# Normalising the query feature map ahead of the numerator matmul, on one core: half the columns there, a new round trip, and a hand-placed order

## The chip, the cores and the metric

One core of one Trainium2 chip. The metric is the device time of one execution in microseconds; lower is better. Most executions of one kernel agree within about 0.3%. The program uses one core only. "Span" is the time from the first to the last recorded instruction; the device time is about 2 us longer.

Engines are named as in the profile: PE is TensorE (matmul), PEld its weight loads, DVE is VectorE, ACT ScalarE, POOL GpSimd, SP the engine that issues most DMAs.

## The reference, cut to what matters

```python
xn = layernorm(x)                                  # x: 2048 tokens x 512
# A: linear attention with 32 heads of 16 ("hedgehog")
q, k, v = split(xn @ wqkv)
pq, pk  = q @ w_phi, k @ w_phi                     # per head, 16 x 16
phi_q   = concat(softmax(pq), softmax(-pq))        # 32 features per head
phi_k   = concat(softmax(pk), softmax(-pk))
kv, z   = phi_k^T @ v, sum over tokens of phi_k
o       = (phi_q @ kv) / (phi_q @ z + 1e-6)
A       = o @ wo
# B: gated unit without an activation
B       = ((xn @ w_gate) * (xn @ w_up)) @ w_down   # F = 1792
out     = x + A + B
```

## The kernel before

All work is in bf16 with f32 accumulation. There are 16 token tiles of 128 (index n) in four groups of 4 (index T). The parts that the change and the argument touch (names are the kernel's own):

```python
# G: one of 56 blocks of the gated unit; ps_gu is a pool of three banks of PSUM, the memory that the matmuls write
gps = ps_gu.tile([P, TT], F32, name="gu")
... 4 matmuls of 512 columns ...
nc.scalar.copy(out=g_sb[:], in_=gps[:])                       # ACT frees the gate's bank
ups = ps_gu.tile([P, TT], F32, name="gu")
... 4 matmuls of 512 columns ...
nc.vector.tensor_tensor(out=hT[T][:, f, :], in0=ups[:], in1=g_sb[:], op=ALU.mult)   # DVE frees it

# Pq: query features of a whole group, features on partitions; NOT normalised
... 4 matmuls: lhsT=W1q, rhs=xnT (512 tokens) ...
nc.scalar.activation(out=Es[T][:, 0, cq, :], in_=pq[:], func=AF.Exp, scale=1.0)
nc.scalar.activation(out=Es[T][:, 1, cq, :], in_=pq[:], func=AF.Exp, scale=-1.0)

# ND: numerator and denominator of one token tile. J = DH + 2 = 18 columns per head:
# 16 of kv, one of z, and one of ones that yields the softmax sum
for cq in range(CQ):
    for s in (1, 0):                                           # exp(-p) and exp(p) apart
        nc.tensor.matmul(nd[...], lhsT=Es[T][:, s, cq, ...], rhs=KVZ[:, s, cq], ...)  # 8 heads x 18 = 144 columns
... DVE: reciprocal (rsm), ratio (rho), multiply (tmp), add (sm), reciprocal (rden) ...
nc.gpsimd.tensor_tensor(out=o_tok, in0=sm, in1=rden, op=ALU.mult)
... o_tok is stored to DRAM (od) and loaded back transposed into oT ...

# KVZ is cleared and its ones are set in the head, on POOL
nc.gpsimd.memset(KVZ[:], 0.0)
... 8 small copies ...
```

The other blocks: LNs, LNr, LNx are the layer norm of a tile (statistics on DVE, rstd on ACT, the scaling on DVE); PK, EX (exps), RED, RCP, PHI (DVE sums, reciprocal, normalising multiply) and VV and KV make kv and z; Fin is the last projection of a tile. In a loop over the key tiles these blocks are mixed with G; then a second loop does ND, the next group's Pq, and G or Fin. Instructions run on each engine in the order in which the program places them.

The softmax here doesn't subtract the row's maximum and nothing guards it: scores larger than these inputs give would overflow.

Of the kernel before, what the change touches and what calls it, by code (L numbers as in the profile page):

```python
# [8 lines left out]
BF16 = mybir.dt.bfloat16  # L9
F32 = mybir.dt.float32  # L10
AF = mybir.ActivationFunctionType
# [10 lines left out]
def kernel(  # L22
# [12 lines left out]
    nc = tc.nc  # L35
# [10 lines left out]
    J = DH + 2  # L46
# [11 lines left out]
    wT_pool = ctx.enter_context(tc.tile_pool(name="wT", bufs=1))  # L58
# [17 lines left out]
    KVZ = wpool.tile([P, 2, CQ, HC, J], BF16, name="KVZ")  # L76
# [8 lines left out]
    wkT = wT_pool.tile([P, DC, D], BF16, name="wT")  # L85
# [7 lines left out]
    nc.sync.dma_start_transpose(out=wkT[:], in_=A_wqkv[:, D:2 * D])  # L93
# [28 lines left out]
    BD = wT_pool.tile([P, DC, HC, DH], BF16, name="BD")  # L122
# [3 lines left out]
    nc.gpsimd.memset(KVZ[:], 0.0)  # L126
    for s in range(2):
        for cq in range(CQ):
            nc.gpsimd.tensor_copy(out=KVZ[:, s, cq, :, DH + 1:DH + 2], in_=BO16[:, :, 0:1])

# [46 lines left out]
    a2e = ctx.enter_context(tc.tile_pool(name="a2e", bufs=2))  # L177
    Es = {}

    def Pq(T, cq, pool, tag):  # L180
        if cq == 0:
            Es[T] = a2e.tile([P, 2, CQ, TT], BF16, name="E")
        pq = pool.tile([P, TT], F32, name=tag, **({"bufs": 2} if tag == "pk" else {}))
        for j in range(DC):
            nc.tensor.matmul(pq[:], lhsT=W1q[:, j, cq * P:(cq + 1) * P], rhs=xnT[:, j, T * TT:(T + 1) * TT],  # L185
                             start=(j == 0), stop=(j == DC - 1))
        nc.scalar.activation(out=Es[T][:, 0, cq, :], in_=pq[:], func=AF.Exp, scale=1.0)  # L187
        nc.scalar.activation(out=Es[T][:, 1, cq, :], in_=pq[:], func=AF.Exp, scale=-1.0)

    with tc.tile_pool(name="ln", bufs=4) as lnpool, \  # L190
# [10 lines left out]
        def LNs(n):  # L201
            ng, ni = divmod(n, GT)
            if ni == 0:
                xns[ng] = xnpool.tile([P, GT, D], BF16, name="xn")
            stats = lnpool.tile([P, nc.vector.BN_STATS_DIM], F32, name="stats")
            nc.vector.bn_stats(out=stats[:], in_=xall[:, n, :])  # L206
            mv = mvs[n] = lnpool.tile([P, nc.vector.BN_AGGR_DIM], F32, name="mv")
            nc.vector.bn_aggr(out=mv[:], in_=stats[:])
# [91 lines left out]

        LNs(0)
# [29 lines left out]
        wqT = wT_pool.tile([P, DC, D], BF16, name="wT")  # L331
        ln_s = [(4, 5), (6, 7)] + [(m,) for m in range(8, 16)] + [(), ()]
        for n in range(NT):
            st = ln_s[min(n + 1, 11)]
            xm = ln_s[min(n, 11)]
            RED(n)
            G()
            if n >= GT:
                VV(n)
            if 12 <= n:  # L340
                foldj(wqT, W1q, n - 12, ps_a1.tile([P, D], F32, name="pk", bufs=2)[:])
            if n > 0:
                KV(n - 1)
            for m in xm:
                LNr(m)
            for m in xm:
                LNx(m)
                if m % 2 == 1:
                    TRst(m)
            if n == 8:  # L350
                nc.sync.dma_start_transpose(out=wqT[:], in_=A_wqkv[:, 0:D])
                nc.sync.dma_start(out=wd[:], in_=B_w_down.rearrange("(c p) d -> p c d", p=P))
                nc.sync.dma_start(out=wo[:], in_=A_wo.rearrange("(c p) n -> p c n", p=P))
            RCP(n)
            PHI(n)
            G()
            for m in st:
                LNs(m)
            if n == GT - 1:
                G()  # L360
            if n + 1 < NT:
                PK(n + 1)
                EX(n + 1)
            if n != GT - 1:
                G(2 if n == 2 else 1 if n < NT - 3 else 0)
        Pq(0, 0, ps_a1, "pk")
        G()
        KV(NT - 1)
        H4 = HC // 2
        kvr = kvt[:].rearrange("p (c r) w -> p c r w", r=2)  # L370
        for s in range(2):
            for r in range(2):
                src, dst = slice(s * HW, (s + 1) * HW), slice(r * HW, (r + 1) * HW)
                mk = BO16[src, s * H4:(s + 1) * H4, :]
                m16 = _bcast_ap(mk, [mk.ap[0], [0, CQ], [DH, H4], [1, DH]])
                m8 = _bcast_ap(mk, [mk.ap[0], [0, CQ], [DH, H4]])
                nc.vector.tensor_tensor(out=KVZ[dst, s, :, r * H4:(r + 1) * H4, 0:DH],
                                        in0=kvr[src, :, r, 0:HW].rearrange("p c (h d) -> p c h d", d=DH),
                                        in1=m16, op=ALU.mult)
                nc.vector.scalar_tensor_tensor(out=KVZ[dst, s, :, r * H4:(r + 1) * H4, DH],  # L380
                                               in0=kvr[src, :, r, HW:HW + 1].to_broadcast((HW, CQ, H4)),
                                               scalar=0.5e-6, in1=m8, op0=ALU.add, op1=ALU.mult)
        Pq(0, 1, ps_a1, "vp")
        Pq(0, 2, ps_a1, "pk")
        Pq(0, 3, ps_gu, "gu")
        G()

    with tc.tile_pool(name="a2s", bufs=2) as a2s, \
            tc.tile_pool(name="a2o", bufs=3) as a2o, \
            tc.tile_pool(name="ps_pq", bufs=1, space=PSUM) as ps_pq, \  # L390
            tc.tile_pool(name="ps_nd", bufs=1, space=PSUM) as ps_nd:
        ods = {}

        def ND(n):
            T, t4 = divmod(n, GT)
            nd = ps_nd.tile([P, 2, 2, 512], F32, name="nd")
            for cq in range(CQ):
                hf, cl = divmod(cq, 2)
                for s in (1, 0):
                    nc.tensor.matmul(nd[:, s, hf, cl * HC * J:(cl + 1) * HC * J],  # L400
                                     lhsT=Es[T][:, s, cq, t4 * P:(t4 + 1) * P],
                                     rhs=KVZ[:, s, cq].rearrange("p h j -> p (h j)"),
                                     start=True, stop=True)
            ndv = [nd[:, s, :, 0:2 * HC * J].rearrange("p a (h j) -> p a h j", j=J) for s in range(2)]
            rsm = a2s.tile([P, 2, 2 * HC, 1], F32, name="rsm")
            nc.vector.reciprocal(out=rsm[:], in_=ndv[1][:, :, :, DH + 1:DH + 2])
            rho = a2s.tile([P, 2, 2 * HC, 1], F32, name="rho")
            nc.vector.tensor_tensor(out=rho[:], in0=ndv[0][:, :, :, DH + 1:DH + 2], in1=rsm[:], op=ALU.mult)
            tmp = a2s.tile([P, 2, 2 * HC, DH + 1], F32, name="tmp")
            nc.vector.tensor_tensor(out=tmp[:], in0=ndv[1][:, :, :, 0:DH + 1],  # L410
                                    in1=rho[:].to_broadcast((P, 2, 2 * HC, DH + 1)), op=ALU.mult)
            sm = a2s.tile([P, 2, 2 * HC, DH + 1], F32, name="sm")
            nc.vector.tensor_tensor(out=sm[:], in0=ndv[0][:, :, :, 0:DH + 1], in1=tmp[:], op=ALU.add)  # L413
            rden = a2s.tile([P, 2, 2 * HC, 1], F32, name="rden")
            nc.vector.reciprocal(out=rden[:], in_=sm[:, :, :, DH:DH + 1])  # L415
            o_tok = a2o.tile([P, D], BF16, name="o_tok")
            nc.gpsimd.tensor_tensor(out=o_tok[:].rearrange("p (a h d) -> p a h d", a=2, d=DH),  # L417
                                    in0=sm[:, :, :, 0:DH],
                                    in1=rden[:].to_broadcast((P, 2, 2 * HC, DH)), op=ALU.mult)
            if t4 == 0:  # L420
                ods[T] = dpool.tile([TT, D], BF16, name=f"od{T}")
            nc.sync.dma_start(out=ods[T][t4 * P:(t4 + 1) * P, :], in_=o_tok[:])
            if t4 == GT - 1:
                nc.sync.dma_start_transpose(out=oT[:, :, T * TT:(T + 1) * TT], in_=ods[T][:])

        fin_next = 0
        for n in range(NT):
            T, t4 = divmod(n, GT)
            ND(n)
            pq = (lambda: Pq(T + 1, t4, ps_pq, "pq")) if T + 1 < NT // GT else None  # L430
            if pq is not None:
                pq()
            if n == GT + 1:
                G()
            if n > GT:
                Fin(fin_next)
                fin_next += 1
            else:
                G(2 if n == 0 else 1)
        while fin_next < NT:  # L440
            Fin(fin_next, 2 if fin_next == NT - 1 else 1)
            fin_next += 1
# [28 lines left out]
```

## Time and profile before

| | before |
|---|---|
| device time, median (lowest to highest, 5 runs) | 227.84 us (227.75 to 228.79) |
| span of the profiled run | 226.1 us |
| PE busy, DVE busy, ACT busy | 97%, 67%, 38% |

From the page of the kernel before: busy time of each engine with its share of the span; then for 40 equal slices of the span the busy tenths of DVE (9 is 90% or more); then the chain of work that ended last, by engine.

```profile
PE 219.5 (97%) x1238; PEld 108.2 (48%) x1261; DVE 152.0 (67%) x263; ACT 86.0 (38%) x177; POOL 22.5 (10%) x42
...
DVE  4769998887779777655877569975555557752121
...
PE 86%; DVE 8%; issue 3%; DMA 1%; ACT 1%; DVEq 0%
```

PE is busy 97% of the span. DVE is full only in six of the slices, three of them early (4 to 6). The chain says what binds: 86% of the span is PE work, and most of the rest is in the head.

A busy PE need not run at its peak, because matmuls are pipelined, so I read PE from start to start in its timeline. Its columns are: start, duration from the first start to the last end, engine, source line, operation, output<-inputs, shape, count. First an ND block and the Pq block after it, then a KV block and the G block after it (kernel before):

```profile
141.36 0.67 PE L400 MATMUL nd<-KVZ,E 128*128 128x144 bf16 x8
141.87 0.81 PE L185 MATMUL pq<-xnT,W1q 128*128 128x512 bf16 x3
```

```profile
95.11 0.42 PE L298 MATMUL kv<-vt,phik 128*128 128x65 bf16 x8
95.37 0.81 PE L151 MATMUL gu<-xnT,wg 128*128 128x512 bf16 x2
```

Four matmuls of 512 columns start every 0.863 us (216 ns each). ND holds PE from 141.36 to 141.87 us, thus 0.50 us for eight matmuls of 144 columns, 62.5 ns each. KV holds it from 95.11 to 95.37, thus 0.26 us for eight of 65 columns.

From the groups of instructions by line and shape (source line, engine, operation, out<-in, shapes, count | busy us, mean ns | idle before, releaser):

```profile
L400 PE MATMUL nd<-KVZ,E 128*128 128x144 bf16 x128 | 10.6, 226 | 0.1
...
L282 DVE TENSOR_REDUCE sums<-e 128x64 f32<-128x1024 f32 x16 | 19.3, 1209 | 3.3 <-ACT e L268 3.3
```

L400 is ND; L282 is RED, which reduces 1024 elements in 1.21 us.

### The profile page before, as it was taken

To read this page: it belongs to the slowest core of one execution; us is meant where nothing else is said; L and a number is where in the kernel's file an instruction comes from. 1 tells how busy PE (TensorE), PEld (TensorE's weight loads), DVE (VectorE), ACT (ScalarE), POOL (GpSimd) and SP (SyncE) were. 2 spreads that over 40 slices of the span, in tenths; PEclk is the share of its full clock that TensorE was granted. 3 is DMA by queue.
4 is the path that set the end of the run, shared out by engine and by line. 5 is a ranking of instruction groups with operands and counts; after the bars stand their busy time and mean duration, and the time that the engine had idled before them with its cause. 6 is when DMAs were issued, how large, how long until landed. Compare 5 with 4: busy or idle time off the path is not lost.

```text
span 226.1 us, 3293 instructions
## 1 busy us (share of the span) xinstructions
PE 219.5 (97%) x1238; PEld 108.2 (48%) x1261; DVE 152.0 (67%) x263; ACT 86.0 (38%) x177; POOL 22.5 (10%) x42
## 2 busy tenths in 40 slices
PE   7899999999999999999999999999999999999994
PEld 2354444444444444445444454544555455554453
DVE  4769998887779777655877569975555557752121
ACT  4575553455454554445455745431111110000000
POOL 6200000000000000000000011330221111130000
PEclk9999999999999999999999999999999999999999
DMA  5999440101407924000000001073142115215201
GB/s 152 268 374 372 138 94 0 51 0 46 93 3 181 339 82 96 0 0 0 4 0 0 0 4 46 31 88 93 46 108 80 46 66 145 74 46 118 69 26 46
DMA packets 33825, 19.38 MB, mean 86 GB/s; under 512 B 20112, under 2 KB 32784, under 8 KB 33808
## 3 DMA queue, kind: packets, MB, share of 16 engines
q1 hardware_dynamic: 33280, 19.14, 30.6%
q8 instruction: 10, 0.16, 0.3%
q10 hardware_dynamic: 528, 0.02, 0.1%
q14 instruction: 7, 0.06, 0.1%
HBM read 8.67 MB, written 5.77 MB: 64 GB/s over the span
## 4 chain that ended last, share of the span: by engine, by line
PE 86%; DVE 8%; issue 3%; DMA 1%; ACT 1%; DVEq 0%
PE gu L169 21%; PE gu L151 18%; PE gu L157 18%; PE gu L172 6%; PE vp L273 5%; PE pk L259 5%; PE pq L185 4%; PE nd L400 4%; DVE hT L159 2%; DVE stats L206 2%; PE kv L298 2%; DVE xn L217 1%; DVE sums L282 1%; DMA xall<-in_A_x_dram 1%; PE pk L185 1%
## 5 line engine op out<-in xcount | busy, mean ns | idle before, releaser
L157 PE MATMUL gu<-xnT,wu 128*128 128x512 bf16 x223 | 57.3, 379 | 0.1
L151 PE MATMUL gu<-xnT,wg 128*128 128x512 bf16 x215 | 56.6, 379 | 0.6
L169 PE MATMUL gu<-wd,hT 128*128 128x512 bf16 (+1 forms) x235 | 50.8, 366 | 0.2
L159 DVE TENSOR_TENSOR hT<-gu,g_sb 128x512 bf16<-128x512 f32 x56 | 38.4, 686 | 15.9 <-PE gu L157 13.3
L154 ACT CAST g_sb<-gu 128x512 bf16<-128x512 f32 x56 | 33.0, 590 | 21.6 <-PE gu L151 21.0
L174 DVE TENSOR_TENSOR o_sb<-gu,xall 128x512 bf16<-128x512 f32 (+1 forms) x17 | 11.2, 660 | 36.2 <-PE gu L172 34.1
L169 PEld LDWEIGHTS <-hT 128*128 128x128 bf16 x238 | 23.1, 98 | 24.4
L417 POOL TENSOR_TENSOR o_tok<-sm,rden 128x512 bf16<-128x512 f32 x16 | 16.9, 1058 | 179.4 <-DVE rden L415 176.1
L157 PEld LDWEIGHTS <-wu 128*128 128x128 bf16 x224 | 21.9, 98 | 26.4
L151 PEld LDWEIGHTS <-wg 128*128 128x128 bf16 x224 | 20.8, 98 | 23.1 <-issue 0.8
L282 DVE TENSOR_REDUCE sums<-e 128x64 f32<-128x1024 f32 x16 | 19.3, 1209 | 3.3 <-ACT e L268 3.3
L187 ACT ACTIVATE E<-pq 128x512 bf16<-128x512 f32 x12 | 7.2, 597 | 35.4 <-PE pq L185 31.2
L293 DVE TENSOR_TENSOR phik<-e,rs 128x1024 bf16<-128x1024 f32 x16 | 19.6, 1225 | 0.5
L267 ACT ACTIVATE e<-pk 128x512 f32<-128x512 f32 x16 | 9.6, 597 | 18.3 <-PE pk L259 17.1
L172 PE MATMUL gu<-wo,xnT 128*128 128x512 bf16 (+1 forms) x66 | 16.3, 366 | 0.1
L259 PE MATMUL pk<-W1k,xnT 128*128 128x512 bf16 x63 | 16.2, 379 | 0.1
L273 PE MATMUL vp<-wv,xnT 128*128 128x512 bf16 x54 | 13.9, 379 | 0.1
L275 ACT CAST vt<-vp 128x512 bf16<-128x512 f32 x14 | 8.2, 587 | 13.8 <-PE vp L273 11.6
L413 DVE TENSOR_TENSOR sm<-nd,tmp 128x544 f32<-128x544 f32 x16 | 11.6, 725 | 1.5
L206 DVE BATCH_NORM_STATS2 stats<-xall 128x6 f32<-128x512 bf16 x16 | 10.8, 678 | 2.2 <-DMA xall<-in_A_x_dram 2.2
L410 DVE TENSOR_TENSOR tmp<-nd,rho 128x544 f32<-128x544 f32 x16 | 11.6, 724 | 0.5
L185 PE MATMUL pq<-xnT,W1q 128*128 128x512 bf16 x43 | 11.7, 379 | 0.2
(63 smaller groups left out, 157.7 us busy)
## 6 DMA issues: line engine op xcount, KB each, us to landing
od<-o_tok SPq DMA_DIRECT2D x16, 128.0 KB, 1.7
out_dram<-o_sb SPq DMA_DIRECT2D x15, 128.0 KB, 1.7
wd<-in_B_w_down_dram SPq DMA_DIRECT2D x1, 1792.0 KB, 10.3
xall<-in_A_x_dram SPq DMA_DIRECT2D x3, 512.0 KB, 12.0
xd<-xn SPq DMA_DIRECT2D x6, 256.0 KB, 2.4
wg<-in_B_w_gate_dram SPq DMA_DIRECT2D x1, 1024.0 KB, 8.3
wu<-in_B_w_up_dram SPq DMA_DIRECT2D x1, 1024.0 KB, 10.5
wv<-in_A_wqkv_dram SPq DMA_DIRECT2D x1, 512.0 KB, 4.8
```

The source lines that it names most:

```text
L151: nc.tensor.matmul(gps[:], lhsT=wg[:, c, f * P:(f + 1) * P], rhs=xnT[:, c, T * TT:(T + 1) * TT], start=(c == 0), stop=(c == DC - 1))
L154: nc.scalar.copy(out=g_sb[:], in_=gps[:])
L157: nc.tensor.matmul(ups[:], lhsT=wu[:, c, f * P:(f + 1) * P], rhs=xnT[:, c, T * TT:(T + 1) * TT], start=(c == 0), stop=(c == DC - 1))
L159: nc.vector.tensor_tensor(out=hT[T][:, f, :], in0=ups[:], in1=g_sb[:], op=ALU.mult)
L169: nc.tensor.matmul(fin[:], lhsT=hT[T][:, f, t4 * P:(t4 + 1) * P], rhs=wd[:, f, sl], start=(f == 0), stop=False)
L172: nc.tensor.matmul(fin[:], lhsT=oT[:, c, n * P:(n + 1) * P], rhs=wo[:, c, sl], start=False, stop=(c == DC - 1))
L185: nc.tensor.matmul(pq[:], lhsT=W1q[:, j, cq * P:(cq + 1) * P], rhs=xnT[:, j, T * TT:(T + 1) * TT], start=(j == 0), stop=(j == DC - 1))
L259: nc.tensor.matmul(pk[:], lhsT=xnT[:, j, n * P:(n + 1) * P], rhs=W1k[:, j, :], start=(j == 0), stop=(j == DC - 1))
L273: nc.tensor.matmul(vp[:], lhsT=xnT[:, j, n * P:(n + 1) * P], rhs=wv[:, j, :], start=(j == 0), stop=(j == DC - 1))
L282: nc.vector.tensor_reduce(out=sums[:], in_=ev, axis=AX.X, op=ALU.add)
L293: nc.vector.tensor_tensor(out=phik[:].rearrange("p k (h f) -> p (k h) f", f=DH), in0=ev, in1=rss[n][:].to_broadcast((P, 2 * H, DH)), op=AL ...
L417: nc.gpsimd.tensor_tensor(out=o_tok[:].rearrange("p (a h d) -> p a h d", a=2, d=DH), in0=sm[:, :, :, 0:DH], in1=rden[:].to_broadcast((P, 2 ...
```

## The change: its intent, and the diff

The intent is to make ND cheaper for PE. Queries are treated as keys already were: tokens on partitions, and normalised before the product. Then exp(p) and the scaled exp(-p) of four heads fill the 128 rows of one weight load, the two halves add up inside the matmul, and the column of ones is not needed: 4 heads x 17 = 68 columns instead of 144. In exchange the features must be transposed, by a store to DRAM and a transposing load (`qd`, `qT`), as o_tok's are. To hide that round trip, and to place the new DVE work, the loops are replaced by one hand-written list of block names. Cut to the core:

```diff
-    J = DH + 2
+    J = DH + 1
-    KVZ = wpool.tile([P, 2, CQ, HC, J], BF16, name="KVZ")
+    KVZ = wpool.tile([P, 2 * CQ, H4, J], BF16, name="KVZ")
-    nc.gpsimd.memset(KVZ[:], 0.0)
-    for s in range(2):
-        for cq in range(CQ):
-            nc.gpsimd.tensor_copy(out=KVZ[:, s, cq, :, DH + 1:DH + 2], in_=BO16[:, :, 0:1])
+    MK = consts.tile([P, H4], BF16, name="MK")          # a mask, used once when KVZ is written
+        def PQ(n):   # 4 matmuls: lhsT=xnT tile, rhs=W1q; then
+            nc.scalar.activation(out=phiq[:, :, 0, :], in_=pqv, func=AF.Exp, scale=1.0)
+            nc.scalar.activation(out=eq[:], in_=pqv, func=AF.Exp, scale=-1.0)
+        def QR(n):
+            nc.vector.tensor_reduce(out=sq[:, 0, :]..., in_=phiqs[n][:, :, 0, :]..., op=ALU.add)
+            nc.vector.tensor_reduce(out=sq[:, 1, :], in_=eqs[n][:]..., op=ALU.add)
+            nc.vector.reciprocal(out=rq[:], in_=sq[:, 1, :])
+            nc.vector.tensor_tensor(out=rho[:]..., in0=sq[:, 0, :], in1=rq[:], op=ALU.mult)
+            nc.gpsimd.tensor_tensor(out=phiqs[n][:, :, 1, :]..., in0=eqs[n][:]..., in1=rho[:]..., op=ALU.mult)
+            nc.sync.dma_start(out=qds[T][...], in_=phiqs[n][:]...)
+            if t4 == GT - 1:                            # two transposing loads per group of four tiles
+                for u in range(2):
+                    nc.sync.dma_start_transpose(out=qTs[T][...], in_=qds[T][...])
+        def ND(n):
+            for i in range(KB):
+                nc.tensor.matmul(nd[:, i, 0:H4 * J], lhsT=qTs[T][:, i, ...], rhs=KVZ[:, i]..., ...)  # 68 columns
+            nc.vector.reciprocal(out=rden[:], in_=ndv[:, :, :, DH:DH + 1])
+            nc.vector.tensor_tensor(out=o_tok[:]..., in0=ndv[:, :, :, 0:DH], in1=rden[:]..., op=ALU.mult)
 ... (the same store and transposing load of o_tok) ...
-        for n in range(NT):  ... the two loops, Pq, the old ND ...
+        for t in (
+            "S6 A1 E0 G W S7 L4 G L5 L6 L7 G C0 G E1 G A2 S8 C1 E2 G K0 G A3 D1 K1 C2 G E3 G L8 "
+ ... (list cut) ...
+            "R7 K13 E15 C15 K14 G G P8 P9 K15 B G N0 G R8 G N1 G G N2 R9 G G N3 G P10 G P11 R10 N4 "
+ ... (list cut) ...
+            "F F F N12 G G N13 G N14 F N15 F F F F F F F ").split():
```

In the list S is LNs, L is LNr and LNx, A is PK and EX, E is RED, C is RCP and PHI, K is KV, V is VV, D a fold of W1q, P is PQ, R is QR, N is ND, F is Fin, B the writing of KVZ, W and X late weight loads.

## The prediction

> **What bounds it now.** TensorE's stream. On the page PE is 97% busy and the chain of waits is 86% PE, at full granted clock. In the timeline of PE, matmuls with 512 columns start 216 ns apart (four take 0.863 us) almost without a break: first G blocks to the last Fin, added up at these intervals, give 207.4 us, and the trace has about 207.8 us. Only some 0.4 us is stall. DVE is busy 67%, ACT 38%, POOL 10%.
>
> **What changes, from TensorE's side.** GLU, Fin, PK, VV, KV, PQ and the folds keep their count and columns. Only ND changes: eight matmuls of 144 columns (0.50 us from first start to the next block's start in the timeline, 62.5 ns each) become eight of 68. KV already runs eight of 65 columns in 0.26 us, so I estimate 0.27 us. Saving: 16 x 0.23 = 3.7 us. The Trainium skill, "TensorE: Matmul & The Clock Gate", section "Back-to-back issue gap", gives N/2.4 + 2.5 ns: 62.5 ns for 144 (the trace agrees) and about 31 ns for 68 (the trace's 32.5 ns for 65 is slightly above). That saving is all on the critical path.
>
> **DVE.** Removed per token tile: two reciprocals, rho, tmp, sm (353+347+191+724+725 ns). Added: two 512-element sums, reciprocal, product (about 1.86 us of DVE time), and in ND a reciprocal and the o_tok multiply (0.98 us). The sums are estimated from the existing 1024-element sum (1209 ns); the skill's "VectorE: DVE Perf Modes", tier table, keeps reductions at 1x whatever the type, so bf16 input doesn't help. DVE busy rises from 152 to about 159 us. POOL keeps a 1.06 us multiply per tile. DMA gains 16 stores and 8 transposes; transposes land in 4 to 6 us now and the list leaves them more.
>
> **Where it could be given back.** The new hand-placed order pulls Q work into the first half. Running sums along the list: DVE work and PE work stay within about 3 us of each other from 15 to 105 us (DVE almost full). At each block that needs a DVE result (PSUM buffers of G, KV after PHI), the largest shortfall is 0.6 us. That assumes DVE never waits; its waits for ACT (rstd up to 1.15 us each before) have no room now, so I add about 1 us. After 110 us DVE has ample room.
>
> **Prediction.** 227.84 - 3.7 + about 1.1 = 225.2 us, range 223.9 to 227.2. Faster by over 2% needs under 223.3 us, more than the whole ND saving, hence 0.07; within 2% 0.90; slower by over 2% 0.03.
>
> **What would show it.** Right: ND's eight matmuls take about 0.27 us; PE's busy time falls by about 4 us in total and every other PE group keeps its mean; the timeline shows a few PE gaps, below 2 us in sum, all between 20 and 105 us, released by DVE (hT) or by ACT behind DVE; DVE over 90% busy there; tail unchanged. Wrong: ND intervals well above 35 ns; PE gaps over 3 us; PE waiting for qT or oT transposes, or for wqT at the first fold; reductions or POOL's multiply clearly slower.
>
> **What would make it wrong.** The queue on SP blocking (phiq stores wait on POOL, transposes on stores) so that late loads reach TensorE late; contention between POOL's strided multiply and DVE; several DVE waits in the full stretch adding up to 3 us or more, leaving no gain.

## The result, and the profile after

| | before | after |
|---|---|---|
| device time, median | 227.84 us (15 runs) | 223.37 us (8 runs, 223.2 to 223.93) |
| ratio, 95% interval | | 0.9794 (0.9778 to 0.981) |
| span of the profiled run | 226.1 us | 221.9 us |
| first G block to the start of the last matmul group | 209.98 us | 205.96 us |

Ratios here are the mean time of one kernel's runs over that of the other's of the same rounds, so not quite the ratio of the medians quoted. Executions over 1.5% slower than the fastest of the same kernel are left out of the means. The gain is 2%, on the edge of what the verdict calls faster (its word here is "unclear" between faster and the same); 223.37 us lies below the predicted range.

The last row of the table is used throughout. I call it the stretch: the time in the PE timeline from the first G matmul to the start of the last group of Fin matmuls. (In every profile the first G group shows three of its four matmuls, as records can be missing, so I put its start one interval, 0.216 us, before the first recorded one.) The stretch leaves out the head, which varies by about a microsecond from run to run, and it repeats well: 205.96 us in three profiles of the changed stream. The two ends, in the kernel before and in the changed kernel (222.64 - 12.88 + 0.216 = 209.98 us; 218.44 - 12.70 + 0.216 = 205.96 us):

```profile
12.88 0.81 PE L151 MATMUL gu<-xnT,wg 128*128 128x512 bf16 x3
...
222.64 0.60 PE L172 MATMUL gu<-wo,xnT 128*128 128x256 bf16 x4
```

```profile
12.70 0.81 PE L151 MATMUL gu<-xnT,wg 128*128 128x512 bf16 x3
...
218.44 0.60 PE L172 MATMUL gu<-wo,xnT 128*128 128x256 bf16 x4
```

The changed kernel's page, the same lines as before:

```profile
PE 215.1 (97%) x1238; PEld 104.6 (47%) x1261; DVE 156.0 (70%) x273; ACT 85.8 (39%) x177; POOL 20.5 (9%) x34
...
DVE  4669999999999999999988696546556136312121
...
PE 95%; DMA 2%; issue 1%; SPq 1%; DVE 0%; ACT 0%; ACTq 0%
```

DVE is now at 9 tenths from slice 4 to slice 20, and PE is as full as before. The chain is 95% PE.

An ND block of the changed kernel in the timeline of PE:

```profile
114.83 0.42 PE L331 MATMUL kv<-KVZ,qT 128*128 128x68 bf16 x8
115.08 1.02 PE L151 MATMUL gu<-xnT,wg 128*128 128x512 bf16 x4
```

ND holds PE for 0.25 to 0.26 us (114.83 to 115.08) instead of 0.50, as estimated from KV. Sixteen times 0.245 us are 3.9 us.

Groups of the changed kernel by line and shape:

```profile
L331 PE MATMUL kv<-KVZ,qT 128*128 128x68 bf16 x128 | 6.7, 194 | 0.0
...
L282 DVE TENSOR_TENSOR phik<-e,rs 128x1024 bf16<-128x1024 f32 x16 | 20.7, 1294 | 0.6
...
L306 DVE TENSOR_REDUCE sq<-phiq 128x32 f32<-128x512 bf16 x16 | 10.8, 675 | 0.0
L309 DVE TENSOR_REDUCE sq<-eq 128x32 f32<-128x512 f32 x16 | 10.8, 675 | 0.0
```

L331 is ND. L306 and L309 are the two new sums; the bf16 one takes 675 ns like the f32 one. The Trainium skill, "VectorE: DVE Perf Modes", section "The perf-mode tier table", lists tensor_reduce at 1x for every type, and the trace agrees. L282 is PHI, 1225 ns on average before and 1294 now (see the end).

Now the full stretch of DVE, by windows (columns: window, its length, then busy us and count of PE, PEld, DVE, ACT, POOL; granted clock; DMA share; GB/s). First the kernel before, then the changed kernel:

```profile
34.00:60.00 26.00, 25.73 (x146) 12.19 (x147) 21.68 (x34) 12.36 (x28) 0.00 (x0) 1.00 0.16 41
60.00:90.00 30.00, 29.84 (x164) 14.20 (x167) 24.50 (x36) 15.54 (x34) 0.00 (x0) 1.00 0.48 132
90.00:105.00 15.00, 14.89 (x86) 7.21 (x87) 9.84 (x13) 7.13 (x13) 0.00 (x0) 1.00 0.00 0
```

```profile
34.00:60.00 26.00, 25.84 (x155) 12.71 (x157) 25.57 (x43) 16.82 (x39) 0.00 (x0) 1.00 0.41 118
60.00:90.00 30.00, 29.84 (x178) 14.41 (x180) 29.28 (x48) 18.42 (x39) 4.24 (x4) 1.00 0.43 105
90.00:105.00 15.00, 14.71 (x88) 7.04 (x88) 14.62 (x22) 8.79 (x17) 2.92 (x3) 1.00 0.10 37
```

From 34 to 105 us DVE is busy 69.5 of 71 us (98%) against 56.0 before. PE's busy time there is the same within 0.1 us. So DVE has filled up and PE has lost nothing.

Was DVE held up by ACT, as I had feared? From the view of who waited for whom (us in total, times, longest), the kernel before and the changed kernel:

```profile
DVE xn L217 <- ACT rstd L213: 6.5, 6, 1.2
```

```profile
DVE xn L206 <- ACT rstd L202: 0.6, 2, 0.3
```

The waits of LNx for rstd did not hurt: they shrank from 6.5 to 0.6 us.

In total: the stretch is 4.02 us shorter. Of that 3.9 us is ND, and the rest, 0.1 us, is all the change that stalls of PE made. An estimate says the same: the matmuls of the built programs in the stretch are 894 of 512 columns, 32 of 256, 16 of 128, 128 of KV and 128 of ND; at the intervals read in the traces (0.863 us for four of 512; 0.109, 0.055 and 0.0325 us for one of the next three; for one of ND 0.0625 before against 0.032 after) they add up to about 209.4 and 205.5 us, so that only some 0.5 us of the stretch is stall, before and after. The median span over all runs of the first batch below is 226.2 us before and 221.4 after, so 4.8 us shorter; 4.0 of them are the stretch and about 0.8 the head. The time outside the span is about 0.2 us longer (223.50 - 221.4 = 2.1 us, against 228.06 - 226.2 = 1.9).

### The profile page after: what moved, and what is told of

It reads as the page before. It is cut to its first block, busy times and chain, and to the rows that moved or that the text cites. A ratio compares the mean times of both kernels' runs of the same rounds, so it can differ in the third digit from the quotient of the medians.

```text
span 221.9 us, 3359 instructions
## 1 busy us (share of the span) xinstructions
PE 215.1 (97%) x1238; PEld 104.6 (47%) x1261; DVE 156.0 (70%) x273; ACT 85.8 (39%) x177; POOL 20.5 (9%) x34
## 4 chain that ended last, share of the span: by engine, by line
PE 95%; DMA 2%; issue 1%; SPq 1%; DVE 0%; ACT 0%; ACTq 0%
PE gu L157 22%; PE gu L169 22%; PE gu L151 21%; PE gu L172 6%; PE pk L295 6%; PE pk L248 6%; PE vp L262 6%; DMA wv<-in_A_wqkv_dram 2%; PE kv L331 2%; PE kv L287 2%; PE pk L262 1%; SPq L81 1%; PE pk L235 1%; PE gu L213 0%; DVE o_sb L174 0%
## 5 line engine op out<-in xcount | busy, mean ns | idle before, releaser
L151 PE MATMUL gu<-xnT,wg 128*128 128x512 bf16 x213 | 55.9, 379 | 0.5
L159 DVE TENSOR_TENSOR hT<-gu,g_sb 128x512 bf16<-128x512 f32 x56 | 37.7, 684 | 9.6 <-PE gu L157 9.5
L316 POOL TENSOR_TENSOR phiq<-eq,rho 128x512 bf16<-128x512 f32 x16 | 17.0, 1060 | 140.9 <-DVE rho L314 69.5
L282 DVE TENSOR_TENSOR phik<-e,rs 128x1024 bf16<-128x1024 f32 x16 | 20.7, 1294 | 0.6
L300 ACT ACTIVATE phiq<-pk 128x512 bf16<-128x512 f32 x16 | 9.6, 598 | 21.5 <-PE pk L295 14.6
L295 PE MATMUL pk<-W1q,xnT 128*128 128x512 bf16 x62 | 16.0, 379 | 0.1
L262 PE MATMUL vp<-wv,xnT 128*128 128x512 bf16 x56 | 14.4, 379 | 1.5 <-DMA wv<-in_A_wqkv_dram 1.2
L337 DVE TENSOR_TENSOR o_tok<-kv,rden 128x512 bf16<-128x512 f32 x16 | 11.1, 691 | 0.6
L306 DVE TENSOR_REDUCE sq<-phiq 128x32 f32<-128x512 bf16 x16 | 10.8, 675 | 0.0
L309 DVE TENSOR_REDUCE sq<-eq 128x32 f32<-128x512 f32 x16 | 10.8, 675 | 0.0
```

The costliest lines, as they stand in the source:

```text
L151: nc.tensor.matmul(gps[:], lhsT=wg[:, c, f * P:(f + 1) * P], rhs=xnT[:, c, T * TT:(T + 1) * TT], start=(c == 0), stop=(c == DC - 1))
L262: nc.tensor.matmul(vp[:], lhsT=xnT[:, j, n * P:(n + 1) * P], rhs=wv[:, j, :], start=(j == 0), stop=(j == DC - 1))
L282: nc.vector.tensor_tensor(out=phik[:].rearrange("p k (h f) -> p (k h) f", f=DH), in0=ev, in1=rss[n][:].to_broadcast((P, 2 * H, DH)), op=AL ...
L295: nc.tensor.matmul(pq[:], lhsT=xnT[:, j, n * P:(n + 1) * P], rhs=W1q[:, j, :], start=(j == 0), stop=(j == DC - 1))
L316: nc.gpsimd.tensor_tensor(out=phiqs[n][:, :, 1, :].rearrange("p k (h f) -> p k h f", f=DH), in0=eqs[n][:].rearrange("p k (h f) -> p k h f" ...
```

## The experiments

Theories. A: PE's stream is the only bound; the gain is ND's columns plus a shorter head, and the full DVE costs nothing because of *when* PE needs its results and which PSUM buffer each G block gets. B, the prediction's: the full DVE stretch costs about 1 us, hidden by something else. Twelve runs. They ran in three batches on three chips, each beside runs of the kernel before: after_again, fixed_rot, dve_less and wv_early; nd128, dve_more, old_order and before_kvz; the other four.

### after_again: the changed kernel once more

No edit.

> The changed kernel once more, as the yardstick for the runs beside it. Every theory: 223.2 to 223.9 us, ratio to the kernel before 0.978 to 0.982. In the profile: first G block at about 12.5 us and the eight ND matmuls about 0.26 us, as in its first profile.

Measured: 223.5 us (223.36 to 224.45), ratio 0.9808 (0.9785 to 0.9831); stretch 205.96 us again. The first G is at 13.0 us instead of 12.5 in the profiled run, because wv landed 0.5 us later. So the head varies and the stretch doesn't: differences of a few tenths are read from the stretch below.

### nd128: is the gain the columns?

```diff
-  nc.tensor.matmul(nd[:, i, 0:H4 * J], ..., rhs=KVZ[:, i]..., ...)           # 68 columns
+  nc.tensor.matmul(nd_flat[i*128 - pad : (i+1)*128 - pad], ..., rhs=KVZ_flat[i*68 - pad : i*68 - pad + 128], ...)
+  # pad is 60 for the last i, else 0; the other 60 columns are never read
```

> The changed kernel with every ND matmul widened from 68 to 128 columns; the additional columns are never read, the result stays right. Theory A (the gain is the columns that TensorE streams in ND): 128 matmuls x 60 columns / 2.4 = 3.2 us more, so about 226.5 us, and ND's eight start within 0.45 us instead of 0.26. Theory B (the gain came from the new order or the head, and short matmuls are bound by something else than columns): under 1 us more.

Measured: 226.48 us (226.36 to 226.57), ratio 0.9918; stretch 209.09 us, 3.13 us more. Result right. An ND block and what follows, in its timeline of PE:

```profile
114.47 0.61 PE L332 MATMUL kv<-KVZ,qT 128*128 128x128 bf16 x8
114.91 1.03 PE L151 MATMUL gu<-xnT,wg 128*128 128x512 bf16 x4
```

Eight matmuls of 128 columns hold PE 0.44 us, 55 ns each. The Trainium skill, "TensorE: Matmul & The Clock Gate", section "Back-to-back issue gap", gives N/2.4 + 2.5 ns as the gap of an isolated matmul, 55.8 ns for 128 columns; the trace agrees with it even in this stream (the page has more for streams, see the end). Columns in ND cost PE their full length, one for one, in the time. Theory A holds for this part.

### dve_less: what does the full DVE cost?

```diff
-  nc.vector.tensor_reduce(out=sq[:, 0, :]..., in_=phiqs[n][:, :, 0, :]..., ...)
-  nc.vector.tensor_tensor(out=rho, in0=sq[:, 0, :], in1=rq[:], op=ALU.mult)
+  nc.vector.tensor_tensor(out=rho, in0=sq[:, 1, :], in1=rq[:], op=ALU.mult)   # wrong result on purpose
```

> Result wrong on purpose: the first of the two sums of each Q tile is left out, 16 x 0.6 us less VectorE work, 11 of it before 111 us. Theory A (TensorE's stream bounds everything, the full VectorE costs next to nothing): VectorE busy falls from 156 to about 145 us and the time falls by at most 0.3 us. Theory B (as predicted: the full VectorE stretch costs about 1 us): the time falls by 0.7 to 1.2 us.

Measured: 223.07 us (223.01 to 223.57), 0.43 us less than after_again, ratio 0.9785. The profiled run's first G was 1.25 us earlier than after_again's (wv had landed earlier), so the time alone can't tell; the stretch is 205.78 us, 0.18 us less. DVE busy fell from 156.0 to 147.6 us. So taking 8.4 us of work from DVE gains the changed kernel about 0.2 us. All stalls of PE in the stretch are some 0.5 us by the estimate above, in both kernels; the prediction had charged 1.1 us more for DVE.

### dve_more: then is DVE far ahead?

```diff
   nc.vector.reciprocal(out=rs[:]..., in_=sums[:])
+  if n in range(4, 14):
+      nc.vector.reciprocal(out=rs[:, 0:H]..., in_=sums[:, 0:H])     # the same values again
```

> The changed kernel with one more 32-element reciprocal on VectorE (0.35 us) after each of ten reciprocals of K tiles 4 to 13, inside the stretch where VectorE is full: 3.5 us more VectorE work. Result right. Theory A (no stall was seen because the list has filled VectorE exactly to what TensorE leaves it, with about 0.5 us to spare): 1.5 to 3.3 us longer, gaps of TensorE at KV and at gates between 60 and 105 us. Theory B (VectorE runs far enough ahead of what TensorE needs from it that its being 98% busy means nothing): at most 0.5 us longer.

Measured: 226.46 us (226.4 to 226.51), ratio 0.9917; stretch 209.08 us, 3.12 us more for about 3.5 us of DVE work. Result right. PE's timeline near the first stalls:

```profile
62.05 1.03 PE L157 MATMUL gu<-xnT,wu 128*128 128x512 bf16 x4
63.66 0.43 PE L289 MATMUL kv<-vt,phik 128*128 128x65 bf16 x8 [0.58 <-DVE phik L284]
```

The KV block should start at 62.91 us, four intervals after 62.05; it starts at 63.66, and the profile names PHI (DVE phik) as what it waited for. In all, the view of waits counts 1.4 us for KV behind PHI in two waits, and 0.2 us for an up group behind an hT. Another 0.9 us, at 103.6 and 105.0 us, are two waits of PE for banks that ACT frees; the first of the exps there had itself waited 2.1 us for PHI. So both statements are true: DVE's load is nearly free as it stands, and there is almost nothing to spare. Ten times 0.35 us came back as 3.1 us. Theory B is wrong about the cost and right about the edge.

### fixed_rot, before_fixed, fixed_less: who frees the PSUM bank

My running sum had found a shortfall of 0.6 us: a gate (the first four matmuls of a G block) needed a bank that DVE had not yet freed. It assumed that the three banks go round in strict turn; then every gate gets the bank of the up matmuls two G blocks earlier, which DVE's hT frees. The trace of the changed kernel contradicts that. PE, then DVE:

```profile
59.82 1.03 PE L151 MATMUL gu<-xnT,wg 128*128 128x512 bf16 x4
...
61.81 1.02 PE L151 MATMUL gu<-xnT,wg 128*128 128x512 bf16 x4
...
64.66 1.03 PE L151 MATMUL gu<-xnT,wg 128*128 128x512 bf16 x3
```

```profile
64.79 1.28 DVE L159 TENSOR_TENSOR hT<-gu,g_sb 128x512 bf16<-128x512 f32 x2
```

The G blocks start at 59.82, 61.81 and 64.66 us. The two hT in the second fence are those of the first two blocks. The earlier one ends at about 65.4 us, but the third block's gate starts at 64.66: it isn't in that bank. The built program says the same; these are rows of its PE order at that block, with the engine that each matmul waits for:

```
584 L151 Matmult gu<-xnT,wg 128x512 [waits Activation_49]
...
592 L157 Matmult gu<-xnT,wu 128x512 [waits DVE_49]
```

The pool handed out a bank that ACT had freed (from the previous gate), and the DVE-freed one went to the up matmuls 0.86 us later. Ten of the 56 gates are served so in the changed kernel, six in the kernel before. The test is to force strict turns, in the changed kernel (fixed_rot), in the kernel before (before_fixed), and together with the lighter DVE (fixed_less):

```diff
-  ps_gu = ctx.enter_context(tc.tile_pool(name="ps_gu", bufs=3, space=PSUM))
+  # three pools' worth of one buffer each, taken in turn by a small wrapper:
+  return ps_gu0.tile(shape, dt, name=f"gu{'abc'[i]}")     # i = 0, 1, 2, 0, ...
```

> The changed kernel with the three PSUM buffers of the G blocks handed out in strict rotation, as my running sum had assumed; in the build as it stands five late gates get a buffer that ScalarE frees instead of one that VectorE frees. Theory A (the hand-out is why the 0.6 us shortfall of the prediction never came): the gate at 30.5 us must now wait for an hT multiply that ended at 30.85 us, the one at 64.66 us for one that ended at 65.40 us, so TensorE stalls by about 0.4 us and 0.8 us in all, and the time is 0.5 to 1.0 us longer than the changed kernel's. Theory B (my VectorE durations were too long and VectorE was simply ahead): no gap, within 0.15 us.

> Control for the strict rotation: the kernel before with its three G buffers handed out in strict rotation. There 6 of 56 gates take a buffer freed by ScalarE, 5 of them in the first 30 us. Theory A (rotation costs only where VectorE is behind, and in the kernel before it is behind for the first 35 us alone): the stretch from first G to last Fin grows from 210.0 us by 0.2 to 1.2 us, less than half of the 2.7 us that rotation cost the changed kernel. Theory B (rotation as such costs, whatever the order): it grows by 2 to 3.5 us.

> Strict rotation and the left-out sum together (result wrong on purpose). Theory A (rotation costs because VectorE is behind when its buffer is due): with 0.6 us less VectorE work per Q tile the cost of rotation shrinks; the stretch from first G to last Fin is 206.2 to 207.7 us, against 208.7 with rotation alone and 205.8 with the lighter VectorE alone. Theory B (rotation costs for another reason): 208.3 us or more.

Measured:

| stretch, us | banks as the build hands them out | strict turns | difference |
|---|---|---|---|
| kernel before | 209.98 | 210.47 (before_fixed) | 0.49 |
| changed kernel | 205.96 | 208.70 (fixed_rot) | 2.74 |
| changed kernel, lighter DVE | 205.78 (dve_less) | 206.20 (fixed_less) | 0.42 |

Times: fixed_rot 226.53 us (226.06 to 227.09), ratio 0.993, 3.0 us over after_again; fixed_less 223.66 us, ratio 0.9834; before_fixed 228.91 us against 227.81 of the kernel before on the same chip, ratio 1.0043 (1.0019 to 1.0067), of which 0.5 us is the stretch; the rest is in the head, whose first G is 0.86 us later in that profile than in the kernel before's. One of fixed_less's six runs took 226.56 us and the others 223.5 to 224.1; the stretch is from one of the others. The same place in fixed_rot, all engines:

```profile
64.57 1.02 PE L257 MATMUL pk<-W1k,xnT 128*128 128x512 bf16 x4
...
65.58 0.68 DVE L168 TENSOR_TENSOR hT<-gub,g_sb 128x512 bf16<-128x512 f32 x1
...
66.31 1.02 PE L160 MATMUL gub<-xnT,wg 128*128 128x512 bf16 x3 [0.71 <-DVE hT L168]
```

PK runs until 65.43 us, and the gate follows only at 66.31, named as waiting 0.71 us for hT, which ran from 65.58 in the bank `gub`. This is exactly the wait that the prediction had foreseen, and more of them came later (at 124, 135 and 165 us): 2.7 us in all, not the 0.5 to 1.0 that I expected. It needs both: strict turns and a DVE that is behind. With 0.6 us less DVE work per query tile it shrinks to 0.4 us, and in the kernel before, whose DVE has room after 35 us, it is 0.5 us.

### old_order: what the list is for

The blocks of the changed kernel, in the order of the kernel before (all key tiles first, then each query tile one group ahead of its ND):

```diff
-  "... L12 K5 P0 S14 S15 G R0 P1 C7 ... B G N0 G R8 G N1 G G N2 ..."
+  "... P0 G K15 B R0 P1 R1 P2 R2 P3 R3 G N0 P4 R4 G G N1 P5 R5 G N2 P6 R6 G N3 P7 R7 G N4 ..."
```

> The arithmetic of the changed kernel, in the order of the kernel before: all K tiles first, then Q tiles one group ahead of their ND. Theory A (the order's part is to hide the new round trip of phi_q: exp, sums, multiply on GpSimd, store, transposing load, some 11 us from the last PQ of a group to its first ND): TensorE waits 5 to 9 us at the ND that opens each of the four groups, and the time is 15 to 35 us longer than the changed kernel's, slower than the kernel before. Theory B (the order matters little, fewer ND columns are the whole change): within 2 us of 223.4 us.

Measured: 283.26 us (283.17 to 284.69), ratio 1.2425. From the view of who waited for whom:

```profile
PE kv L331 <- DMA qT<-qd: 48.5, 8, 13.8
DVE xn L206 <- ACT rstd L202: 6.7, 7, 1.2
```

PE waits 48.5 us in eight waits for the transposing load, up to 13.8 us each; I had expected 5 to 9 us each and 15 to 35 in all. The mean granted clock of PE fell to 0.897 in this run, with slices at about half clock after the gaps; that may be part of the 11 us that these waits don't explain. In this order the round trip costs far more than ND's columns are worth. The list avoids that by starting the queries long before ND needs them (in the changed kernel the first PQ is at 54.6 us, the first ND at 111.1), and so their sums fall into the stretch in which DVE is full. The second line is used below: with the same blocks in the old order, DVE waits 6.7 us for rstd again.

### before_kvz: where the head's part comes from

The head of the kernel before, DVE, POOL and PE:

```profile
4.82 1.73 DVE L217 TENSOR_SCALAR xn<-xall,mv,rstd 128x512 bf16<-128x512 bf16 x2
5.02 1.06 POOL L126 MEMSET KVZ<- 128x1152 bf16 x1
...
6.28 0.71 PE L224 MATMUL gu<-ident,xn 128*128 128x128 bf16 x8 [0.88 <-DVE xn L217]
```

Two LNx took 1.73 us, and POOL cleared KVZ at the same time. Of all 16 LNx (count, then shortest, median and longest in ns, first and last start in us), the longest is this first one, from 4.82 to 6.23 us:

```profile
L217 DVE TENSOR_SCALAR xn<-xall,mv,rstd x16: 395/412/1410, 4.8 to 82.0; 128x512 bf16<-128x512 bf16 x16
```

The same place after the change, where KVZ isn't cleared:

```profile
4.69 0.41 DVE L206 TENSOR_SCALAR xn<-xall,mv,rstd 128x512 bf16<-128x512 bf16 x1
...
5.18 0.39 PE L213 MATMUL gu<-ident,xn 128*128 128x128 bf16 x4
...
7.70 1.02 PE L262 MATMUL vp<-wv,xnT 128*128 128x512 bf16 x4 [1.25 <-DMA wv<-in_A_wqkv_dram]
```

LNx takes 0.41 us, and the first transposes start at 5.18 us instead of 6.28. The test moves only that clearing in the kernel before:

```diff
+  nc.gpsimd.memset(KVZ[:], 0.0)        # and the 8 copies: now ahead of the four BD multiplies
   BD = ...; 4 x nc.gpsimd.tensor_tensor(out=BD[:, c], ...)
-  nc.gpsimd.memset(KVZ[:], 0.0)        # and the 8 copies
```

> The kernel before with only one thing changed: GpSimd's clearing and marking of KVZ is moved ahead of the BD multiplies, so that it is over before the first LNx. Theory A (GpSimd's memset held back the two LNx of the head, 1.3 us instead of 0.41 us): the first two LNx take about 0.41 us each, the first transposes start at about 5.2 us instead of 6.28, then the load of wv limits as in the changed kernel, the first G block starts 0.1 to 0.3 us earlier, and the time falls by 0.1 to 0.4 us. Theory B (they were slow for another reason): LNx stays at over 0.6 us, head and time the same.

Measured: 227.43 us (227.07 to 229.33) against 228.04 of the kernel before, ratio 0.9977 (0.9928 to 1.0025): the time doesn't settle it, as one of four runs was at 229.33. (The other three have spans of 225.4 to 225.7 us, below all seven of the kernel before beside it, 225.9 to 227.2; that hints at about half a microsecond and doesn't show it.) The trace shows what moved in the head:

```profile
2.42 1.06 POOL L122 MEMSET KVZ<- 128x1152 bf16 x1
...
4.60 1.09 DVE L217 TENSOR_SCALAR xn<-xall,mv,rstd 128x512 bf16<-128x512 bf16 x2
...
5.25 0.90 PE L224 MATMUL gu<-ident,xn 128*128 128x128 bf16 x8 [0.48 <-DVE xn L217]
...
7.55 0.59 PE L273 MATMUL vp<-wv,xnT 128*128 128x512 bf16 x2 [1.19 <-DMA wv<-in_A_wqkv_dram]
```

With the memset over by 3.5 us, both LNx together take 1.09 us (the first 0.59, the second 0.41, both beside BD multiplies) and the transposes start at 5.25. Then PE waits for wv until 7.55 us. The stretch is 209.94 us, unchanged. The Trainium skill, "SBUF — State Buffer", section "Who interferes with whom", says that VectorE in a two-port mode, which a tensor_scalar such as LNx can enter, and GpSimd contend for a shared port pair: whoever issues first has it for the whole instruction, and the other fully blocks. The trace agrees that the two collide: the first LNx of the kernel before took 1.41 us and ended 0.15 us after the memset, while the memset took 1.06 us, as in before_kvz. It does not bear out the rest: by the records LNx had started 0.20 us before the memset and yet was the one held up, and 0.15 us after the memset is less than its whole length of 0.41 us. Spans on POOL are rough, and a BD multiply ran there until 5.09 us, so who issued first stays open.

So the removed memset lets the first transposes start 1.1 us earlier, and the load of wv takes a part of that back. How large its net share of the gain is was not settled by a time, and that it is the cause of the shorter head is argued, not shown; the spans' medians put the head's whole part at about 0.8 us.

### wv_early, head1, head2: attempts at a faster version

The head now waits for wv. Three edits tried to move it: wv second on ACT's queue (wv_early); the second x tile on ACT's queue, so that SP issues wv 0.47 us sooner (head1); and head1 with wv in two halves whose first half is used at once for two tiles (head2).

```diff
 # wv_early
+  dma_cols(wv, A_wqkv, 2 * D, 0, D, nc.scalar)    # right after wphi; the issue on SP is removed
 # head1
-  dma_x(1, 2)
+  nc.scalar.dma_start(out=xall[:, 1:2, :], in_=x_view[:, 1:2, :])
 # head2, also
+  for c in range(0, DC, 2):  nc.sync.dma_start(out=wv[:, c:c + 2, :], ...)
+  VVh(0, vp0, (0, 1)); VVh(1, vp1, (0, 1)); VVh(0, vp0, (2, 3)); ...
```

> The changed kernel with the load of wv issued second on the queue of ScalarE instead of fourth on that of SP. In the changed kernel's profile TensorE waits 1.25 us for wv (it lands at 7.66 us) although its other operand was ready at 6.2 us. Theory A (that load ate what the shorter head of the change had gained): wv lands before 6.6 us, the first VV block starts at 6.2 to 6.8 us, the first G block about 0.5 to 0.8 us earlier than 12.48 us, and the time falls by as much. Theory B (something else limits the head just behind it: the transposed wk, the first columns of wg, or the tiles of x now landing later): the first G moves by under 0.2 us and the time is the same.

> The changed kernel with the second x tile loaded from ScalarE's queue, so that SP issues tiles 2 and 3 and wv 0.45 us earlier without putting wv ahead of them (the run with wv early moved the wait from wv to those tiles). Theory A (issue order on SP sets the head): wv lands about 0.4 us earlier than the 6.7 to 8.2 us seen, first G at 11.6 to 12.3 us, time 223.0 us or a little less, stretch from first G to last Fin unchanged at 206.0 us. Theory B (the landing of wv is set by what the 16 DMA engines carry, not by issue): first G within the 12.0 to 13.2 us seen, same time.

> head1, and wv loaded in two halves, with the first half of VV of tiles 0 and 1 run before the second half is needed. Theory A: TensorE starts VV at 6.2 to 6.8 us and fills the wait for the second half with 0.86 us of matmuls; first G 0.4 to 1.0 us earlier than in the changed kernel, time 222.4 to 223.0 us, faster than both kernels. Theory B (tiles 2 and 3, or the transposed wk, or the first columns of wg limit next): first G no earlier than in head1.

Measured: wv_early 224.21 us (ratio 0.9829), head1 223.86 us (0.9823), head2 223.72 us (0.9814); stretches 205.96, 206.00 and 205.98 us. None is faster than the changed kernel (223.37 and 223.5). In wv_early:

```profile
6.32 1.04 PE L262 MATMUL vp<-wv,xnT 128*128 128x512 bf16 x4
6.63 0.69 DVE L195 BATCH_NORM_STATS2 stats<-xall 128x6 f32<-128x512 bf16 x1 [0.87 <-DMA xall<-in_A_x_dram]
...
8.69 0.40 PE L213 MATMUL gu<-ident,xn 128*128 128x128 bf16 x4 [1.34 <-DVE xn L206]
```

The first VV starts at 6.32 us as hoped, but the statistics of the third x tile wait for its load until 6.63, and PE's next transposes come at 8.69, after 1.34 us of idleness. In head1 and head2 the second x tile lands at 4.5 us, and its layer norm and transposes come ahead of the first VV, which starts at 6.99 and 6.93. Each edit gave one load less delay and another one more. The first G started at 12.63 us in wv_early, 12.33 in head1 and 12.07 in head2, all within the 11.7 to 13.0 us that profiles with the changed kernel's own head show. For wv_early and head1 that is what theory B expected, though wv_early's time is 0.7 us over after_again's; in head2 the first G is a little earlier than in head1, against B, and the time is not the 222.4 to 223.0 us of theory A. That the amount to be loaded sets the head, and not the order in which it is asked for, fits these runs and is not shown. No version that beats the changed kernel came of this.

## Why the prediction was right or wrong, point by point

- "That saving is all on the critical path", 3.7 us for ND: right. Measured 3.9 us (0.245 instead of 0.23 us per block), and nd128 gave 3.13 us back for 60 of the 76 columns, which is the same rate.
- "DVE busy rises from 152 to about 159 us": it is 156.0. The sums at 1x and POOL's multiply (1.06 us) were right.
- "DVE almost full" from 15 to 105 us: right, 98% from 34 to 105.
- "At each block that needs a DVE result ... the largest shortfall is 0.6 us": **wrong, the first failed step.** It took a rule for the buffers that the build doesn't follow (strict turns; the text of fixed_rot's expectation names it). The gate at which the sum had its shortfall starts at 64.66 us without waiting. Forcing the rule costs 2.74 us, so the sum was also too small for the case that it assumed.
- "its waits for ACT ... have no room now, so I add about 1 us": **wrong, the second failed step.** The waits for rstd fell from 6.5 to 0.6 us, and in old_order, with the same blocks, they are back at 6.7 us: it is the list that removed them. My reading is that a DVE that works through a backlog finds its inputs ready, so that the same time was counted twice, as backlog and as waiting; no run tests that alone. Together the two terms were "+ about 1.1"; the runs show about -0.1 us in the stretch, and 0.2 us that 8.4 us less work on DVE would still gain.
- The head was taken as unchanged ("tail unchanged" and no term for the head): a term was missing. The diff removes POOL's clearing of KVZ, and the profile of before showed LNx at up to 1.41 us beside it against 0.41 elsewhere. It may well be the main part of a head that is about 0.8 us shorter. The time outside the span grew by about 0.2 us; why is open.
- The sum as it should have stood: 227.84 - 3.9 (ND) - 0.1 (stalls) - 0.8 (head) + 0.2 (outside the span) = 223.2 us, against 223.37 measured. Taking out the 1.1 alone would have left 224.1 us; the head is the other part of the miss.
- "contention between POOL's strided multiply and DVE" as a risk: it is there and cheap. The changed kernel's timeline, POOL and DVE:

```profile
60.93 1.06 POOL L316 TENSOR_TENSOR phiq<-eq,rho 128x512 bf16<-128x512 f32 x1 [55.78 <-ACT vt L264]
61.29 1.79 DVE L282 TENSOR_TENSOR phik<-e,rs 128x1024 bf16<-128x1024 f32 x1
```

PHI takes 1.79 us here instead of 1.22, and ends 1.09 us after POOL's multiply does. It happens to two of sixteen PHI, the two that POOL's multiply overlaps (0.7 us each); the others take 1.22 to 1.23 us.
- "Faster by over 2% needs under 223.3 us, more than the whole ND saving": right as arithmetic; with the head's part the result came within 0.1 us of that line.

## What to carry to other kernels

Here an engine that was 98% busy beside a full TensorE cost only what TensorE waited for at single blocks: before charging for it, look up which buffer each block gets and which engine frees it, in the build and not from a rule, and ask whether the waits of today will be there in the new order before adding them. Then test the edge from both sides, lighter and heavier; here the lighter side was worth 0.2 us and 3.5 us more of work cost 3.1. When a diff removes an instruction from an engine that "doesn't matter", look at what ran slowly beside it.

## What the Trainium skill lacked or had wrong

- "TensorE: Matmul & The Clock Gate", section "Back-to-back issue gap", says that in a real stream of weight loads and matmuls 512 columns sustain about 131 ns per matmul, and 128 columns about 81 ns, and that N/2.4 + 2.5 over-counts at 512. Here such streams run at 216 ns for 512 columns (four in 0.863 us, each with its weight load) and at 55 ns for 128 columns (nd128). The simple formula fits; the sustained figures are not seen.
- The same section's formula gives 29.6 and 30.8 ns for 65 and 68 columns; KV and ND measured 32.5 and 32 ns (0.26 us and 0.255 us for eight). A small excess at short matmuls, for which the page gives no size at these lengths.
- "SBUF — State Buffer", section "Who interferes with whom", was right that VectorE and GpSimd collide; it gives no size for a case like this one, and that whoever issues first keeps the ports for the whole instruction isn't what the records show. Here a POOL memset of 1152 bf16 elements stretched a 0.41 us LNx to 1.41 us, although LNx had started 0.20 us earlier, and a 1.06 us POOL multiply made a 1.22 us multiply of DVE with two SBUF inputs take 1.79 us.
- I found no page that says how a full, in-order engine beside a full TensorE is to be costed: its waits shrank from 6.5 to 0.6 us here, and which engine frees the next PSUM buffer decided 2.7 us.
- I found no page on the spread of one load's landing between executions of the same program: wv, 512 KB, took 4.5 to 6.0 us from issue to landing in the profiles of kernels with the same head, and the first G started between 11.7 and 13.0 us.
